# Linear attention with a highway feed-forward: the key turns moved a whole iteration ahead of their scores, to the head of the TensorE sequence

## The chip, the cores and the metric

The kernel runs on one core of a Trainium2 chip. The time is that of the device in microseconds (us), from runs of the whole program; the profile comes from one further execution. TensorE (PE) multiplies matrices into PSUM, VectorE (DVE) and ScalarE (ACT) read PSUM and write SBUF, GpSimd (POOL) works in SBUF alone, and SyncE (SP) issues the DMAs. Each engine takes its instructions in the sequence in which the program wrote them, and waits for the others on semaphores.

## The reference

Attention with a decay per head, in blocks, and behind it a highway layer. Cut to what matters (q, k, v are 4 x 8 x 768 x 64, 3072 tokens of width 512):

```python
for b in range(nb):
    intra = einsum(qb, kb) * Dmask          # lam ** (i - j) where i >= j
    intra = einsum(intra, vb)
    inter = einsum(qb * lam_pow, kv_state)
    out[b] = intra + inter
    kv_state = lam_block * kv_state + einsum(kb * rev_pow, vb)
x = out.transpose(0, 2, 1, 3).reshape(B * S, H * D)
H = maximum(x @ w_h, 0)
T = 1 / (1 + exp(-(x @ w_t + b_t)))
return T * H + (1 - T) * x
```

Inputs and output are float32; the kernel multiplies in bf16.

## The kernel before, in words

**Tiling.** The kernel takes chunks of 128 tokens with all eight heads: 24 chunks (N), six for each of the four batch entries (NCH). The powers of the decay are not in the masks: V is scaled by a power for its position (`scale_v`, L143), the result by one for the query's position (`intra`, L202), so the mask is a plain triangle. Two chunks form a group of 256 tokens for the feed-forward; the last two chunks are groups of their own.

**Steps of a chunk n.** POOL casts the keys to bf16 (`cast_k`, L138) and scales V (L145); queries are cast for two chunks at a time (`cast_q`, L153). PE turns the keys, four 128x128 transposes into the PSUM tile "tr" (`trans_k`, L166), and ACT copies them to `kT` (L168). Queries go the same way for two chunks at a time, eight transposes into a tile of the same name and one ACT copy (`trans_q`, L159 and L161). Both share the one PSUM buffer of "tr". `scores` (L179) multiplies turned queries and keys, eight matmuls, and DVE masks the result (L182). `inter` (L189) is the product with the state so far, four matmuls, left out for the first chunk of a batch entry; `intra` (L196) adds the masked scores times V, eight matmuls, and DVE writes the result as xT (L202). `state` (L211) updates the state with four matmuls, and ACT copies it in two halves to `s_bd` (L215); it is left out for the last chunk of a batch entry.

**Feed-forward.** A group is worked off in two units of half the output columns. `ffn_step` takes one unit: eight matmuls for H (`h_ps`, L223; DVE makes hmx from it, L226), then, if a finished chunk waits, its output (`ffn_out`: eight matmuls into `x_ps`, L250, an ACT copy to `o_sb`, L254, and a DMA, L257), then eight matmuls for T (`t_ps`, L235), two sigmoids on ACT (L239) and a DVE product (`thmx`, L242). PSUM has one buffer for each of these tiles.

**Sequence.** The sequence is the one in which the code is written; there is no scheduler. The first two chunks are worked off ahead of the loop, with the two units of the first group. Iteration i of the loop holds: POOL's casts for chunk i + 3; inter(i); scores(i + 1); intra(i) and state(i); in even iterations the query turns for chunks i + 2 and i + 3; one `ffn_step`; the key turns for chunk i + 2; the loads for chunk i + 10. The scores of chunk i + 2 stand in iteration i + 1, with inter(i + 1) alone between the turns and them on PE. From iteration 24 on there are only feed-forward units and outputs left.

**Buffers.** Loads have ten buffers for each of k and v and five for the query pairs; `kb` and `vs` four, `kT` three, `qT` and `qb` two, `o_sb` six.

Of the kernel before, what the change touches and what calls it, by code (L numbers as in the profile page):

```python
# [16 lines left out]
def kernel(  # L17
# [19 lines left out]
    N = B * NCH  # L37
# [100 lines left out]
    def cast_k(n, eng=None):  # L138
        kb[n] = work.tile([C, H, D], BF16, tag="kb", name="kb", bufs=4)
        (eng or nc.gpsimd).tensor_copy(kb[n], kf[n])  # L140

    def scale_v(n):
        c = n % NCH  # L143
        vs[n] = work.tile([C, H, D], BF16, tag="vs", name="vs", bufs=4)
        nc.gpsimd.tensor_tensor(vs[n], in0=vf[n], in1=pow_k[:, :, c, :].to_broadcast([C, H, D]), op=ALU.mult)  # L145

    def cast_q(s, engs=None):
        qb[s] = work.tile([128, J, H, D], BF16, tag="qb", name="qb")
        engs = engs or [nc.gpsimd]
        w = H // len(engs)  # L150
        for i, eng in enumerate(engs):
            h = slice(i * w, i * w + w)
            eng.tensor_copy(qb[s].rearrange("p j h d -> p h j d")[:, h], qf[s].rearrange("p h (j d) -> p h j d", j=J)[:, h])  # L153

    def trans_q(s):
        tr = ps.tile([128, NP, J, 128], BF16, tag="tr", name="tr")
        for hp in range(NP):
            for j in range(J):
                nc.tensor.transpose(tr[:, hp, j, :], qb[s][:, j, 2 * hp:2 * hp + 2, :], id128)  # L159
        qT[s] = work.tile([128, NP, J * C], BF16, tag="qT", name="qT")  # L160
        nc.scalar.activation(qT[s].rearrange("p n (q j) -> p n q j", j=J), tr.rearrange("p n j q -> p n q j"), AF.Copy)  # L161

    def trans_k(n):
        tr = ps.tile([128, NP, C], BF16, tag="tr", name="tr")
        for hp in range(NP):
            nc.tensor.transpose(tr[:, hp, :], kb[n][:, 2 * hp:2 * hp + 2, :], id128)  # L166
        kT[n] = work.tile([128, NP, C], BF16, tag="kT", name="kT", bufs=3)
        nc.scalar.activation(kT[n], tr, AF.Copy)  # L168

    def q_of(n, r, hp):  # L170
        o = n % J * C
        return qT[n // J][r, hp, o:o + C]

    def scores(n):
        s_ps = ps.tile([C, 2, NP, C], F32, tag="s", name="s_ps")
        for hp in range(NP):
            for e in range(2):
                r = slice(64 * e, 64 * e + 64)
                nc.tensor.matmul(s_ps[:, e, hp, :], lhsT=kT[n][r, hp, :], rhs=q_of(n, r, hp), start=True, stop=True)  # L179
        masked[n] = work.tile([C, 2, NP, C], BF16, tag="masked", name="masked")  # L180
        for e in range(2):
            nc.vector.tensor_tensor(masked[n][:, e], in0=s_ps[:, e],  # L182
                                    in1=tri.to_broadcast([C, NP, C]), op=ALU.mult)

    def inter(n):
        o_ps[n] = ps.tile([128, NP, C], F32, tag="o", name="o_ps")
        if n % NCH:
            for hp in range(NP):
                nc.tensor.matmul(o_ps[n][:, hp, :], lhsT=s_bd[n % 2][:, hp, :], rhs=q_of(n, slice(0, 128), hp),  # L189
                                 start=(hp == 0), stop=False, skip_group_check=True)  # L190

    def intra(n):
        c = n % NCH
        for hp in range(NP):
            for e in range(2):
                nc.tensor.matmul(o_ps[n][64 * e:64 * e + 64, hp, :], lhsT=vs[n][:, 2 * hp + e, :], rhs=masked[n][:, e, hp, :],  # L196
                                 start=(hp == 0 and c == 0), stop=True, skip_group_check=True)
        g = group[n]
        r = n - first[g]
        if r == 0:  # L200
            xT[g] = work.tile([128, NP, sizes[g] * C], BF16, tag=f"xT{sizes[g]}", name="xT", bufs=3)
        nc.vector.tensor_tensor(xT[g][:, :, r * C:(r + 1) * C], in0=o_ps[n], in1=pow_q[:, :, c * C:(c + 1) * C], op=ALU.mult)  # L202

    def state(n):
        b, c = divmod(n, NCH)
        if c == NCH - 1:
            return
        if c == 0:
            kv_ps[b] = ps.tile([128, NP, 128], F32, tag="kv", name="kv_ps")
        for hp in range(NP):  # L210
            nc.tensor.matmul(kv_ps[b][:, hp, :], lhsT=kb[n][:, 2 * hp:2 * hp + 2, :], rhs=vs[n][:, 2 * hp:2 * hp + 2, :],  # L211
                             start=(c == 0 and hp == 0), stop=True, skip_group_check=True)
        for e in range(2):
            r = slice(64 * e, 64 * e + 64)
            nc.scalar.activation(s_bd[(n + 1) % 2][r, :, r], kv_ps[b][r, :, r], AF.Copy)  # L215


    def ffn_h(g, js):
        T = sizes[g] * C
        h_ps = ps.tile([128, len(js), T], F32, tag="h", name="h_ps")  # L220
        for i, j in enumerate(js):
            for kc in range(KC):
                nc.tensor.matmul(h_ps[:, i, :], lhsT=wh[:, kc, j * 128:(j + 1) * 128], rhs=xT[g][:, kc, :],  # L223
                                 start=(kc == 0), stop=(kc == KC - 1))
        hmx = work.tile([128, len(js), T], BF16, tag=f"hmx{len(js)}", name="hmx")
        nc.vector.scalar_tensor_tensor(hmx, in0=h_ps, scalar=0.0, in1=xT[g][:, js[0]:js[-1] + 1, :],  # L226
                                       op0=ALU.max, op1=ALU.subtract)
        return hmx

    def ffn_t(g, js, hmx):  # L230
        T = sizes[g] * C
        t_ps = ps.tile([128, len(js), T], F32, tag="t", name="t_ps")
        for i, j in enumerate(js):
            for kc in range(KC):
                nc.tensor.matmul(t_ps[:, i, :], lhsT=wt[:, kc, j * 128:(j + 1) * 128], rhs=xT[g][:, kc, :],  # L235
                                 start=(kc == 0), stop=(kc == KC - 1))
        t_sb = work.tile([128, len(js), T], BF16, tag=f"t_sb{len(js)}", name="t_sb")
        for i, j in enumerate(js):
            nc.scalar.activation(t_sb[:, i, :], t_ps[:, i, :], AF.Sigmoid, bias=bt_col[:, j:j + 1])  # L239
        if js[0] == 0:  # L240
            thmx[g] = work.tile([128, NP, T], BF16, tag=f"thmx{sizes[g]}", name="thmx")
        nc.vector.tensor_tensor(thmx[g][:, js[0]:js[-1] + 1, :], in0=t_sb, in1=hmx, op=ALU.mult)  # L242

    def ffn_out(n, eng="act"):
        g = group[n]
        r = n - first[g]
        x_ps = ps.tile([C, DM], F32, tag="x", name="x_ps")
        for j in range(NP):
            for i, t in enumerate((xT[g], thmx[g])):
                nc.tensor.matmul(x_ps[:, j * 128:(j + 1) * 128], lhsT=t[:, j, r * C:(r + 1) * C], rhs=id128,  # L250
                                 start=(j == 0 and i == 0), stop=(i == 1), skip_group_check=True)
        o_sb = work.tile([C, DM], F32, tag="o_sb", name="o_sb", bufs=6)
        if eng == "act":
            nc.scalar.activation(o_sb, x_ps, AF.Copy)  # L254
        else:
            nc.vector.tensor_copy(o_sb, x_ps)  # L256
        nc.sync.dma_start(out=out[n * C:(n + 1) * C, :], in_=o_sb)  # L257
# [3 lines left out]
    def ffn_step(eng="act"):  # L261
        unit = units.pop(0) if units else None
        if unit:
            hmx = ffn_h(*unit)
        if outs:
            ffn_out(outs.pop(0), eng)
        if unit:
            ffn_t(*unit, hmx)
            g, js = unit
            if js[-1] == NP - 1:  # L270
                outs.extend(range(first[g], first[g] + sizes[g]))
# [31 lines left out]
    cast_q(1)  # L303
    scale_v(2)
    ffn_step()
    ffn_step()
    trans_k(2)
    trans_q(1)
    scores(2)
    cast_k(3)  # L310
    scale_v(3)
# [8 lines left out]
    i = 2  # L320
    while i < N or units or outs:
        if i + 3 < N:
            cast_k(i + 3)
            scale_v(i + 3)
            if i % J and (i + 3) % J == 0:
                cast_q((i + 3) // J)
        if i < N:
            inter(i)
        if i + 1 < N:
            scores(i + 1)  # L330
        if i < N:
            intra(i)
            state(i)
        if i % J == 0 and i + 2 < N:
            trans_q(i // J + 1)
        ffn_step("dve" if i >= N and i % 2 else "act")
        if i < N:
            close(i)
        if i + 2 < N:
            trans_k(i + 2)  # L340
        loads(i + LA)
        i += 1

# [29 lines left out]
```

## Time and profile before

| | us |
|---|---|
| median of 3 runs (lowest to highest) | 141.66 (141.54 to 141.77) |
| the profiled execution | 141.39 |
| its span, from the first to the last instruction | 139.6 |
| PE busy | 102.9 |
| ACT busy | 81.2 |
| DVE busy | 77.8 |
| POOL busy | 55.3 |

The mean granted TensorE clock was 0.959 of full speed. The kernel moved 27.48 MB. The span is shorter than the profiled execution's time by 1.8 us, which lie around the first and the last instruction. A row of the timeline gives start, duration, engine, line and operation, what it writes and reads, how many such instructions are merged in the row, and in brackets the engine's idle time ahead of it with what ended it. Matmul durations include the pipeline's depth, so that the pitch of a series is read from start to start.

### The profile page before, as it was taken

What the parts mean: (1) busy time and instruction counts of PE and PEld (TensorE: products, weight loads), DVE (VectorE), ACT (ScalarE), POOL (GpSimd) and SP (SyncE); (2) the same over time, 40 slices, a digit from 0 to 9 for tenths busy, and PEclk for the clock granted to TensorE, in tenths of its full rate; (3) what the DMA queues carried; (4) which work ended last, traced back from release to release, by engine and by line L of the source; (5) the groups of instructions that cost most, each with busy time, mean ns of one, the idle gap of its engine ahead of it and who ended that gap; (6) DMA issues with size and microseconds to landing.
All of it is one profiled execution on the core that took longest, in us unless ns stands there. A gap on an engine that the chain in (4) does not pass through costs nothing.

```text
span 139.6 us, 3394 instructions
## 1 busy us (share of the span) xinstructions
PE 102.9 (74%) x1345; PEld 85.8 (61%) x1345; DVE 77.8 (56%) x135; ACT 81.2 (58%) x165; POOL 55.3 (40%) x73
## 2 busy tenths in 40 slices
PE   0257893789976887797779779778867977799950
PEld 0144572577755775686568569557756865688840
DVE  4316832625657595476477447645854774674351
ACT  3756946184543855846656567559368566745540
POOL 5076357382919391545336237337325400000000
PEclk9999999655899999999999999999999999999998
DMA  1999999999998999999999999998122022102323
GB/s 41 275 257 368 303 233 236 217 217 243 246 219 210 247 275 260 225 258 258 288 267 262 254 267 261 270 284 241 50 80 75 0 75 80 71 6 86 144 79 146
DMA packets 67175, 27.48 MB, mean 197 GB/s; under 512 B 50772, under 2 KB 63064, under 8 KB 67160
## 3 DMA queue, kind: packets, MB, share of 16 engines
q1 hardware_dynamic: 67008, 27.27, 81.4%
q8 instruction: 10, 0.16, 0.5%
q14 instruction: 5, 0.04, 0.1%
q10 hardware_dynamic: 152, 0.01, 0.1%
HBM read 20.98 MB, written 6.29 MB: 195 GB/s over the span
## 4 chain that ended last, share of the span: by engine, by line
PE 60%; ACT 24%; DVE 6%; DMA 4%; issue 3%; SPq 0%; ACTq 0%
PE t_ps L235 15%; PE h_ps L223 14%; ACT t_sb L239 13%; ACT kT L168 8%; PE s_ps L179 8%; PE x_ps L250 7%; PE o_ps L196 6%; PE kv_ps L211 5%; PE tr L159 5%; DMA qf<-in_q_dram 4%; DVE masked L182 3%; ACT qT L161 2%; DVE o_sb L256 1%; ACT o_sb L254 1%; DVE w_b L294 1%
## 5 line engine op out<-in xcount | busy, mean ns | idle before, releaser
L182 DVE TENSOR_TENSOR masked<-s_ps,tri 128x512 bf16<-128x512 f32 x48 | 30.9, 686 | 19.9 <-PE s_ps L179 19.6
L145 POOL TENSOR_TENSOR vs<-vf,pow_k 128x512 bf16<-128x512 f32 x24 | 25.6, 1067 | 18.0 <-DMA vf<-in_v_dram 10.2
L215 ACT ACTIVATE s_bd<-kv_ps 64x256 bf16<-64x256 f32 x40 | 15.1, 378 | 25.8 <-PE kv_ps L211 25.3
L242 DVE TENSOR_TENSOR thmx<-t_sb,hmx 128x512 bf16<-128x512 bf16 x24 | 11.0, 459 | 30.7 <-ACT t_sb L239 30.7
L239 ACT ACTIVATE t_sb<-t_ps,bt_col 128x256 bf16<-128x256 f32 (+1 forms) x52 | 20.8, 455 | 11.7 <-PE t_ps L235 11.7
L179 PE MATMUL s_ps<-qT,kT 64*128 64x128 bf16 x192 | 10.6, 236 | 21.9 <-ACT kT L168 18.8
L223 PE MATMUL h_ps<-xT,w_b 128*128 128x256 bf16 (+1 forms) x208 | 25.8, 270 | 0.4 <-DVE xT L202 0.4
L235 PE MATMUL t_ps<-xT,w_b 128*128 128x256 bf16 (+1 forms) x208 | 25.5, 268 | 0.1
L140 POOL CAST kb<-kf 128x512 bf16<-128x512 f32 x23 | 14.1, 614 | 26.7 <-issue 18.0
L179 PEld LDWEIGHTS <-kT 64*128 64x128 bf16 x192 | 6.2, 101 | 26.1 <-ACT kT L168 23.5
L223 PEld LDWEIGHTS <-w_b 128*128 128x128 bf16 x208 | 18.5, 100 | 2.8 <-issue 0.6
L235 PEld LDWEIGHTS <-w_b 128*128 128x128 bf16 x208 | 18.7, 100 | 2.2 <-issue 0.2
L254 ACT ACTIVATE o_sb<-x_ps 128x512 f32<-128x512 f32 x22 | 13.1, 595 | 9.9 <-PE x_ps L250 9.8
L226 DVE SCALAR_TENSOR_TENSOR hmx<-h_ps,xT 128x512 bf16<-128x512 f32 x24 | 16.4, 684 | 2.3 <-PE h_ps L223 1.5
L202 DVE TENSOR_TENSOR xT<-o_ps,pow_q 128x512 bf16<-128x512 f32 x24 | 16.3, 680 | 0.7 <-PE o_ps L196 0.7
L153 POOL CAST qb<-qf 128x1024 bf16<-128x1024 f32 (+1 forms) x12 | 12.5, 1040 | 7.7 <-DMA qf<-in_q_dram 7.7
L250 PE MATMUL x_ps<-id,xT 128*128 128x128 bf16 x96 | 14.2, 227 | 1.3 <-ACT o_sb L254 0.7
L168 ACT ACTIVATE kT<-tr 128x512 bf16<-128x512 bf16 x24 | 14.3, 596 | 1.2 <-PE tr L166 1.1
L250 PE MATMUL x_ps<-id,thmx 128*128 128x128 bf16 x96 | 14.2, 227 | 0.2 <-DVE thmx L242 0.2
L161 ACT ACTIVATE qT<-tr 128x1024 bf16<-128x1024 bf16 x12 | 12.3, 1024 | 2.7 <-PE tr L159 2.4
L196 PE MATMUL o_ps<-masked,vs 128*64 128x128 bf16 x192 | 11.4, 241 | 0.8 <-DVE masked L182 0.8
L250 PEld LDWEIGHTS <-thmx 128*128 128x128 bf16 x96 | 9.8, 102 | 2.1 <-DVE thmx L242 1.2
(42 smaller groups left out, 97.9 us busy)
## 6 DMA issues: line engine op xcount, KB each, us to landing
kf<-in_k_dram SPq DMA_DIRECT2D x24, 256.0 KB, 4.9
qf<-in_q_dram SPq DMA_DIRECT2D x12, 512.0 KB, 5.7
vf<-in_v_dram SPq DMA_DIRECT2D x24, 256.0 KB, 5.7
out_dram<-o_sb SPq DMA_DIRECT2D x24, 256.0 KB, 4.5
w_f<-in_moe_w_h_dram SPq DMA_DIRECT2D x4, 256.0 KB, 4.5
w_f<-in_moe_w_t_dram SPq DMA_DIRECT2D x4, 256.0 KB, 5.3
lam_bc<-in_lam_dram ACTq DMA_DIRECT2D x1, 4.0 KB, 3.1
bt_r<-in_moe_b_t_dram ACTq DMA_DIRECT2D x1, 2.0 KB
```

What stands on the lines that cost most here:

```text
L145: nc.gpsimd.tensor_tensor(vs[n], in0=vf[n], in1=pow_k[:, :, c, :].to_broadcast([C, H, D]), op=ALU.mult)
L168: nc.scalar.activation(kT[n], tr, AF.Copy)
L179: nc.tensor.matmul(s_ps[:, e, hp, :], lhsT=kT[n][r, hp, :], rhs=q_of(n, r, hp), start=True, stop=True)
L182: nc.vector.tensor_tensor(masked[n][:, e], in0=s_ps[:, e], in1=tri.to_broadcast([C, NP, C]), op=ALU.mult)
L196: nc.tensor.matmul(o_ps[n][64 * e:64 * e + 64, hp, :], lhsT=vs[n][:, 2 * hp + e, :], rhs=masked[n][:, e, hp, :], start=(hp == 0 and c == 0 ...
L202: nc.vector.tensor_tensor(xT[g][:, :, r * C:(r + 1) * C], in0=o_ps[n], in1=pow_q[:, :, c * C:(c + 1) * C], op=ALU.mult)
L215: nc.scalar.activation(s_bd[(n + 1) % 2][r, :, r], kv_ps[b][r, :, r], AF.Copy)
L223: nc.tensor.matmul(h_ps[:, i, :], lhsT=wh[:, kc, j * 128:(j + 1) * 128], rhs=xT[g][:, kc, :], start=(kc == 0), stop=(kc == KC - 1))
L226: nc.vector.scalar_tensor_tensor(hmx, in0=h_ps, scalar=0.0, in1=xT[g][:, js[0]:js[-1] + 1, :], op0=ALU.max, op1=ALU.subtract)
L235: nc.tensor.matmul(t_ps[:, i, :], lhsT=wt[:, kc, j * 128:(j + 1) * 128], rhs=xT[g][:, kc, :], start=(kc == 0), stop=(kc == KC - 1))
L239: nc.scalar.activation(t_sb[:, i, :], t_ps[:, i, :], AF.Sigmoid, bias=bt_col[:, j:j + 1])
L250: nc.tensor.matmul(x_ps[:, j * 128:(j + 1) * 128], lhsT=t[:, j, r * C:(r + 1) * C], rhs=id128, start=(j == 0 and i == 0), stop=(i == 1), s ...
```

## The change

Two calls move. In the loop, the key turns of chunk i + 2 (`trans_k(i + 2)`) stood behind the feed-forward unit of iteration i, and now stand at its head, ahead of inter(i). The scores of chunk i + 2 stay in iteration i + 1. Ahead of the loop, the turns of keys 2 and of the second query pair stood behind the two feed-forward units of the first group, and now stand between them.

```diff
     scale_v(2)
     ffn_step()
-    ffn_step()
     trans_k(2)
     trans_q(1)
+    ffn_step()
     scores(2)
...
                 cast_q((i + 3) // J)
+        if i + 2 < N:
+            trans_k(i + 2)
         if i < N:
             inter(i)
         if i + 1 < N:
...
         if i < N:
             close(i)
-        if i + 2 < N:
-            trans_k(i + 2)
         loads(i + LA)
```

PE in the steady loop, before: the end of iteration 7 and iteration 8 up to its query turns. One row stands for each series of four or eight matmuls. Numbers tell the buffers apart: kb_686 holds the keys of chunk 9, kT_860 their turned copy, made from tr_855.

```order
L235 MATMUL t_ps_842<-xT_562,w_b1_90 128x256
L166 MATMUL tr_855<-id128_135,kb_686 128x128
L189 MATMUL o_ps_870<-qT_729,s_bd0_158 128x128
L179 MATMUL s_ps_875<-qT_729,kT_860 128x128
L196 MATMUL o_ps_870<-masked_801,vs_621 64x128
L211 MATMUL kv_ps_713<-vs_621,kb_619 128x128
L159 MATMUL tr_903<-id128_135,qb_785 128x128
```

The same place after the change; the keys of chunk 9 (kb_686) were turned at the head of iteration 7, which is the row at the top, and kb_781 holds those of chunk 10.

```order
L166 MATMUL tr_787<-id128_135,kb_686 128x128
L235 MATMUL t_ps_849<-xT_569,w_b1_90 128x256
L166 MATMUL tr_870<-id128_135,kb_781 128x128
L189 MATMUL o_ps_877<-qT_736,s_bd0_158 128x128
L179 MATMUL s_ps_882<-qT_736,kT_792 128x128
L196 MATMUL o_ps_877<-masked_808,vs_621 64x128
L211 MATMUL kv_ps_720<-vs_621,kb_619 128x128
L159 MATMUL tr_910<-id128_135,qb_785 128x128
```

The series have the same sequence of kinds here; what moved is the chunk that is turned. Iteration 8's scores read kT_792, turned in iteration 7's head, and the turns that stand in front of them are for the scores of iteration 9.

ACT at the same place, before and then after:

```order
L239 ACTIVATE t_sb_851<-t_ps_842,bt_col_171 128x256 x2
L168 ACTIVATE kT_860<-tr_855 128x512
L215 ACTIVATE s_bd1_160<-kv_ps_713 64x4x64 x2
L161 ACTIVATE qT_912<-tr_903 128x1024
L254 ACTIVATE o_sb_934<-x_ps_925 128x512
```

```order
L239 ACTIVATE t_sb_858<-t_ps_849,bt_col_171 128x256 x2
L168 ACTIVATE kT_875<-tr_870 128x512
L215 ACTIVATE s_bd1_160<-kv_ps_720 64x4x64 x2
L161 ACTIVATE qT_919<-tr_910 128x1024
L254 ACTIVATE o_sb_941<-x_ps_932 128x512
```

ACT's sequence of kinds is the same in the loop; the key copy behind the sigmoids is that of chunk 10 and no longer that of chunk 9. DVE, POOL and SP have the same sequences before and after.

## Prediction

> **What bounds the kernel now.** I read the page first, for what is busy and what the chain that ended last is made of. Rows of section 2 (40 slices of 3.5 us: TensorE busy, granted TensorE clock, DMA) and of section 4:
>
> ```profile
> PE   0257893789976887797779779778867977799950
> PEclk9999999655899999999999999999999999999998
> DMA  1999999999998999999999999998122022102323
> PE 60%; ACT 24%; DVE 6%; DMA 4%; issue 3%; SPq 0%; ACTq 0%
> ```
>
> No engine is full. The DMA engines are loaded until slice 27 (about 97 us) and nearly idle afterwards, yet PE shows the same 7 to 8 tenths before and after that point: in the second half it isn't the loads that hold PE. ACT carries 24% of the chain. The view of waits says where PE stops for ACT:
>
> ```profile
> PE s_ps L179 <- ACT kT L168: 18.8, 20, 1.2
> ```
>
> The scores wait 20 times for the copy of the turned keys. One iteration of the loop shows how. PE from the timeline (start, duration, engine, line; matmuls are pipelined, so I count from start to start), then ACT in the same stretch:
>
> ```profile
> 54.97 0.61 PE L159 MATMUL tr<-id,qb 128*128 128x128 bf16 x8
> 55.41 1.04 PE L223 MATMUL h_ps<-xT,w_b 128*128 128x256 bf16 x8
> 56.29 0.22 PE L250 MATMUL x_ps<-id,xT 128*128 128x128 bf16 x1
> ...
> 56.73 1.04 PE L235 MATMUL t_ps<-xT,w_b 128*128 128x256 bf16 x8
> 57.61 0.39 PE L166 MATMUL tr<-id,kb 128*128 128x128 bf16 x4
> 57.83 0.39 PE L189 MATMUL o_ps<-qT,s_bd 128*128 128x128 bf16 x4
> 59.19 0.40 PE L179 MATMUL s_ps<-qT,kT 64*128 64x128 bf16 x8 [0.97 <-ACT kT L168]
> 59.52 0.41 PE L196 MATMUL o_ps<-masked,vs 128*64 128x128 bf16 x8
> 59.86 0.40 PE L211 MATMUL kv_ps<-vs,kb 128*128 128x128 bf16 x4
> 60.10 1.04 PE L223 MATMUL h_ps<-xT,w_b 128*128 128x256 bf16 x8
> ```
>
> ```profile
> 57.81 0.84 ACT L239 ACTIVATE t_sb<-t_ps,bt_col 128x256 bf16<-128x256 f32 x2 [0.26 <-PE t_ps L235]
> 58.54 0.60 ACT L168 ACTIVATE kT<-tr 128x512 bf16<-128x512 bf16 x1
> ```
>
> PE turns the keys at 57.61 and runs the state product at 57.83; those four matmuls end their issue at about 58.05 (four of them took 0.22 at 57.61). ACT is busy with two sigmoids until 58.65, then copies kT until 59.14, and the scores start at 59.19. So PE issues nothing for 59.19 - 58.05 = 1.14 us in each iteration. The path is PE's FFN, ACT's sigmoids, ACT's kT, PE's scores, and round again.
>
> Up to about 50 us something else holds too. POOL's casts of the queries (start, duration; the first row is the scaling of V ahead of one):
>
> ```profile
> 34.35 1.06 POOL L145 TENSOR_TENSOR vs<-vf,pow_k 128x512 bf16<-128x512 f32 x1 [2.55 <-DMA vf<-in_v_dram]
> 35.35 1.04 POOL L153 CAST qb<-qf 128x1024 bf16<-128x1024 f32 x1
> 42.67 1.04 POOL L153 CAST qb<-qf 128x1024 bf16<-128x1024 f32 x1
> 49.34 1.23 POOL L153 CAST qb<-qf 128x1024 bf16<-128x1024 f32 x1
> ```
>
> POOL waits for V there, and the pairs of queries are ready at 36.39, 43.71 and 50.57, 7.3 and 6.9 us apart. No order on PE brings these forward.
>
> **The pre-loop edit** puts the second pair's turns between the two FFN units. PE's waits there now, and the cast that iteration 2 needs:
>
> ```profile
> 22.78 0.61 PE L159 MATMUL tr<-id,qb 128*128 128x128 bf16 x8 [1.19 <-ACT kT L168]
> 24.50 0.40 PE L179 MATMUL s_ps<-qT,kT 64*128 64x128 bf16 x8 [1.11 <-ACT qT L161]
> ```
>
> ```profile
> 26.88 1.04 POOL L153 CAST qb<-qf 128x1024 bf16<-128x1024 f32 x1 [2.14 <-DMA qf<-in_q_dram]
> ```
>
> The second unit's matmuls would lie beside these copies, so up to 2.3 us of waits can go. I cost it at nothing, because the query turns of iteration 2 need the cast that ends at 27.92, and those of iteration 4 the one that ends at 36.39: what is gained ahead is waited away there.
>
> **The loop edit** moves four turns per iteration and one ACT copy; it adds and removes no instruction, and neither SP's, POOL's nor DVE's sequence changes. The scores of iteration i now read a kT copied a whole iteration earlier, so the 1.14 us goes. What is late next, in the order of the iteration, counted from the turns at its head:
>
> PE's own pitch, from the rows above: turns 0.22, state product 0.22, scores 0.33, intra 0.34, state update 0.24, h 0.88, x 0.44, t 0.88, together 3.55 us; the query turns of even iterations 0.44.
>
> The turned tiles share one PSUM buffer ("tr", one buffer). The query turns now come 1.35 us after the key turns (0.22 + 0.22 + 0.33 + 0.34 + 0.24), and the kT copy ends 59.14 - 57.61 = 1.53 after them, since ACT still does the sigmoids first; with 0.05 to pass the signal (59.14 to 59.19) the query turns can start at 1.58. So 0.23 of the wait comes back in each even iteration. This is a new wait, and h, x and t stand behind it. An even iteration is then 1.58 + 0.44 + 0.88 + 0.44 + 0.88 = 4.22, a pair 7.77. Where a chunk is the last of its batch the state update (0.24) is left out, in odd iterations only; where it is the first, the state product is left out, which the new wait swallows.
>
> VectorE, from the same stretch:
>
> ```profile
> 59.63 1.29 DVE L182 TENSOR_TENSOR masked<-s_ps,tri 128x512 bf16<-128x512 f32 x2 [0.52 <-PE s_ps L179]
> 60.84 0.68 DVE L202 TENSOR_TENSOR xT<-o_ps,pow_q 128x512 bf16<-128x512 f32 x1
> 61.43 0.68 DVE L226 SCALAR_TENSOR_TENSOR hmx<-h_ps,xT 128x512 bf16<-128x512 f32 x1
> 63.36 0.42 DVE L242 TENSOR_TENSOR thmx<-t_sb,hmx 128x512 bf16<-128x512 bf16 x1 [1.25 <-ACT t_sb L239]
> ```
>
> After the change the sigmoids end 1.04 after the head (57.81 + 0.84 - 57.61); thmx then ends at 1.46, masked at 2.75, xT at about 3.4, hmx at about 4.0. The next state product needs xT's PSUM tile at 3.55 + 0.22 = 3.77: 0.4 us of slack. The next h, at 3.55 + 1.35 = 4.9, needs hmx: 0.9. So DVE does not bind, but the first margin is small. ACT: the kT copy is done by 1.53, before the state update's result can arrive; its longest sequence in an even iteration ends before the next sigmoids.
>
> **The sum.** Iteration 4's query turns start when their cast is done, 36.39 and 0.05 for the signal, say 36.45. From there to those of iteration 6 PE has 0.44 + 0.88 + 0.88 (no x yet), an iteration without state update and x, 2.87, and 1.58: 43.10, and it waits for the cast until 43.76. To iteration 8: 2.64 + 3.55 + 1.58, so 51.53, now behind PE and not behind the cast (50.57). Before, this point was 54.97: 3.44 gained. From there to the start of h in iteration 22, the last with scores: six pairs less two state updates, 6 x 7.77 - 0.48 = 46.14, then 2.64 + 3.55 and 1.13 (no turns in iteration 22), 53.46 together. It starts at 104.99. Before:
>
> ```profile
> 123.21 1.04 PE L223 MATMUL h_ps<-xT,w_b 128*128 128x256 bf16 x8
> ```
>
> That is 18.2 us earlier, and behind it the same work follows as before (16.4 us to the end of the span, 139.6). The profiled execution took 141.39, so 123.2; the median of the runs is 141.66, 0.27 above it: 123.4.
>
> Does the DMA allow it? SP's issues in sequence, and the time to landing:
>
> ```profile
> 62.41 0.59 SPq L55 DMA_DIRECT2D kf<-in_k_dram  x1
> 88.14 1.52 SPq L60 DMA_DIRECT2D vf<-in_v_dram  x1
> 89.75 1.05 SPq L257 DMA_DIRECT2D out_dram<-o_sb  x1
> 90.89 0.39 SPq L55 DMA_DIRECT2D kf<-in_k_dram  x1
> ```
>
> ```profile
> vf<-in_v_dram SPq DMA_DIRECT2D x24, 256.0 KB, 5.7
> out_dram<-o_sb SPq DMA_DIRECT2D x24, 256.0 KB, 4.5
> ```
>
> SP issues without a pause here: seven chunks with their outputs in 90.89 - 62.41 = 28.48 us, 4.07 each, slower than the 3.85 that PE would now take. PE starts with a lead to spend. The queries for iteration 20 come after the V issued at 88.14: 93.8 landed, 1.06 and 1.04 on POOL, 95.9; PE wants them at 51.53 + 46.14 = 97.7. The output buffers (six) tell the same: the o_sb of iteration 19 needs the output issued at 89.75 gone, 94.3, and ACT wants it at about 95.4. Margins of 1 to 2 us: the loads nearly bind, and a floor follows. At 95.9 instead of 97.7 the whole would be 121.6.
>
> **The clock.** The granted clock in stretches (fields: window, length, busy of PE, PEld, DVE, ACT, POOL, clock, DMA share, GB/s):
>
> ```profile
> 24.00:26.00 2.00, 0.95 (x16) 0.67 (x15) 1.06 (x2) 1.05 (x2) 0.73 (x2) 0.94 1.17 256
> 34.00:36.00 2.00, 1.66 (x22) 1.20 (x22) 0.19 (x1) 1.08 (x2) 1.65 (x2) 0.50 1.33 217
> 36.00:38.00 2.00, 2.00 (x31) 1.74 (x26) 1.72 (x4) 1.29 (x3) 2.00 (x4) 1.00 1.12 254
> ```
>
> PE ran at half clock from about 26 to 36 us, and came back as FFN matmuls began. After the change PE waits for the cast of 36.39. If the half clock of some 9.5 us fell behind that wait, it would cost 4.7 us of work, less the 0.66 in hand before 43.76: about 4.1. If it stays ahead of it, nothing. I take 0.9, nearer to nothing, because in the trace the clock is back at once with the FFN. Sum: 124.3.
>
> The Trainium skill (TensorE: Matmul & The Clock Gate, "HAM oscillation — how this bites in real kernels") says that an idle gap of PE of over about 3.4 us drops the clock to half; this speaks against the change, which makes PE reach its wait sooner. By that page, as an estimate, one window of 3.4 us at half clock behind the wait would lose 1.7 us of work, and the sum would be 124.4 rather than the 123.4 without any loss. The 0.50 at 34 to 36 us agrees with a halved clock; that the waits quoted ahead of it are 1.19 us at most doesn't.
>
> **Rivals.**
> *The DMA becomes the bound* (15 in 100). For it: 4.07 against 3.85, margins under 2 us. Against: what is issued, and in which sequence, stays. If the loads from 51 us on came a tenth slower, the last queries would be 4.4 us later, 100.3 instead of 97.7 wanted; with the 0.9 about 127, and with outputs delayed likewise up to 130.
> *Half of the wait returns elsewhere* (12 in 100): in-line waits on ACT or DVE, such as xT's with its 0.4 us of slack. 14 iterations x 0.57 = 8 us: 132.
> *The wait isn't worth its time* (2 in 100): another round (sigmoid, thmx, masked, xT) has the same length and takes its place. Then about 141.6. The DVE's 0.52 and 1.25 us of idle time in that round speak against it.
> *Slower* (3 in 100): PE reaches waits for loads so often that the clock stays at half. An iteration then takes about 3.85 longer. The gain of 18.2 is lost when 18.2 / 3.85, some five iterations, run so, that is 37 us at half clock beyond those of now. From 36 to 85 us it would cost 24: about 148. The clock of 1.00 with waits of 1.14 us per iteration now speaks against it.
>
> **How the numbers follow.** The forecast has 68 in 100, 124.3, and by itself spans 122 to 126.5 (no clock term and loads at their floor, to most of the 4.1). With the DMA rival the range is 122 to 130 for 83 in 100. Faster by over 0.2% (what a measurement here can tell): 68 + 15 + 12 = 95; within it 2; slower 3.
>
> **What would show it.** The next query turns of before, for the pitch:
>
> ```profile
> 64.78 0.61 PE L159 MATMUL tr<-id,qb 128*128 128x128 bf16 x8
> ```
>
> Right: the wait of the scores for kT is gone (18.8 us to under 3); a new one of the query turns for kT of about 0.2 in each even iteration; pairs of iterations of about 7.7 us where 9.8 stood (54.97 above to the row below); h of iteration 22 near 105; the last key load issued at about 91 as now. Wrong: waits of PE for POOL's kb or qb behind 51 us (the DMA rival), waits for xT (the second), or 0.50 in the clock row behind 40 us (the last).

## The result and the profile after

The changed kernel took 125.66 us in the median of 4 runs (124.51 to 126.75), beside 141.6 for the kernel before; the ratio is 0.885, with a 95% interval of 0.877 to 0.893. The profiled execution took 125.1 us with a span of 123.3. A second series gave 126.03 in the median of 6 (ratio 0.887, 0.882 to 0.891). The prediction said 124.3, with a range of 122 to 130. Ratios and their intervals leave out runs over 1.5% slower than the fastest of the same kernel; the medians count every run.

The same rows of the page as shown of before (TensorE busy, granted clock, DMA, by engine on the chain that ended last):

```profile
PE   0236896756819999999999999999999999999930
PEclk9999999999985999999999999999999999999996
DMA  1999999998999999899999999999999972222233
PE 57%; SPq 18%; DMA 8%; ACT 6%; DVE 4%; issue 2%; POOL 2%; POOLq 0%
```

PE is now at 9 tenths from slice 13 (from about 37 us) to slice 38 (about 117 us), where it stood at 7 to 8. ACT has gone from 24% of the chain to 6%. What holds the end now is PE's own sequence behind about 37 us, and ahead of it the loads, which stand as SPq and DMA. In the view of waits, over the whole span, those of PE for casts and for turned copies:

```profile
PE tr L159 <- POOL qb L153: 3.4, 2, 2.5
PE tr L159 <- ACT kT L168: 1.7, 4, 1.2
PE s_ps L179 <- ACT qT L161: 1.1, 1, 1.1
```

The 18.8 us of the scores waiting for kT are gone altogether. The 1.1 us of the last row and 1.2 of the 1.7 us for kT stand ahead of the loop. Inside it, query turns wait for the cast (0.85 and 2.51 us), and three times, up to 0.19 us, for the kT copy to leave the shared PSUM buffer. One pair of iterations on PE, from the timeline:

```profile
52.59 0.61 PE L159 MATMUL tr<-id,qb 128*128 128x128 bf16 x8
...
55.22 0.39 PE L166 MATMUL tr<-id,kb 128*128 128x128 bf16 x4
55.45 0.39 PE L189 MATMUL o_ps<-qT,s_bd 128*128 128x128 bf16 x4
55.77 0.40 PE L179 MATMUL s_ps<-qT,kT 64*128 64x128 bf16 x8
56.09 0.41 PE L196 MATMUL o_ps<-masked,vs 128*64 128x128 bf16 x8
...
58.87 0.39 PE L166 MATMUL tr<-id,kb 128*128 128x128 bf16 x4
...
60.45 0.61 PE L159 MATMUL tr<-id,qb 128*128 128x128 bf16 x8
...
63.08 0.39 PE L166 MATMUL tr<-id,kb 128*128 128x128 bf16 x4
```

The scores start 0.32 us behind the state product, without a wait. The odd iteration takes 58.87 - 55.22 = 3.65, the even one 63.08 - 58.87 = 4.21, the pair 7.86, where it was 9.8. The query turns come 60.45 - 58.87 = 1.58 behind the key turns, as forecast for the shared buffer.

The steps of the sum against two profiles of the changed kernel (in brackets with the clock term of 0.9):

| start, us | forecast | first profile | second profile |
|---|---|---|---|
| query turns, iteration 4 | 36.45 | 36.58 | 36.65 |
| query turns, iteration 6 | 43.76 (44.66) | 44.73 | 44.31 |
| query turns, iteration 8 | 51.53 (52.43) | 52.59 | 52.19 |
| query turns, iteration 20 | 97.67 (98.57) | 99.46 | 99.77 |
| h, iteration 22 | 104.99 (105.89) | 106.97 | 107.28 |
| end of the span | 121.4 (122.3) | 123.3 | 123.6 |

At iteration 8 the sum with the clock term holds to 0.25 us; at iteration 6 it is 0.07 short in the first profile and 0.35 long in the second, where the clock did not fall. From iteration 8 to iteration 22 it is short by 0.9 in the first profile and 1.6 in the second.

### The profile page after: what moved, and what is told of

The parts are those of the page before. It is cut to its first block, busy times and chain, and to the rows that moved or that the text cites. A ratio compares the mean times of both kernels' runs of the same rounds, so it can differ in the third digit from the quotient of the medians.

```text
span 123.3 us, 3388 instructions
## 1 busy us (share of the span) xinstructions
PE 101.0 (82%) x1345; PEld 84.1 (68%) x1345; DVE 79.5 (64%) x135; ACT 81.9 (66%) x165; POOL 56.4 (46%) x73
## 4 chain that ended last, share of the span: by engine, by line
PE 57%; SPq 18%; DMA 8%; ACT 6%; DVE 4%; issue 2%; POOL 2%; POOLq 0%
PE h_ps L223 14%; PE t_ps L235 14%; SPq L60 9%; PE x_ps L250 7%; SPq L55 6%; DMA vf<-in_v_dram 5%; PE tr L159 5%; PE o_ps L196 4%; ACT t_sb L239 4%; PE s_ps L179 4%; DMA w_f<-in_moe_w_h_dram 4%; PE kv_ps L211 3%; PE o_ps L189 3%; SPq L65 2%; PE tr L166 2%
## 5 line engine op out<-in xcount | busy, mean ns | idle before, releaser
L242 DVE TENSOR_TENSOR thmx<-t_sb,hmx 128x512 bf16<-128x512 bf16 x24 | 15.4, 643 | 21.1 <-ACT t_sb L239 20.9
L223 PE MATMUL h_ps<-xT,w_b 128*128 128x256 bf16 (+1 forms) x208 | 26.7, 276 | 0.2 <-POOL w_b L300 0.2
L223 PEld LDWEIGHTS <-w_b 128*128 128x128 bf16 x208 | 18.8, 101 | 2.9 <-issue 0.4
L235 PEld LDWEIGHTS <-w_b 128*128 128x128 bf16 x208 | 18.9, 100 | 2.2
L153 POOL CAST qb<-qf 128x1024 bf16<-128x1024 f32 (+1 forms) x12 | 13.1, 1088 | 8.0 <-DMA qf<-in_q_dram 8.0
L250 PE MATMUL x_ps<-id,xT 128*128 128x128 bf16 x96 | 13.4, 219 | 1.3 <-ACT o_sb L254 0.7
L250 PE MATMUL x_ps<-id,thmx 128*128 128x128 bf16 x96 | 13.4, 219 | 0.2 <-DVE thmx L242 0.2
L159 PE MATMUL tr<-id,qb 128*128 128x128 bf16 x96 | 8.2, 233 | 6.3 <-POOL qb L153 3.4
L159 PEld LDWEIGHTS <-qb 128*128 128x128 bf16 x96 | 6.6, 103 | 7.9 <-POOL qb L153 4.5
L166 PE MATMUL tr<-id,kb 128*128 128x128 bf16 x96 | 9.8, 227 | 2.3 <-DVE kb L140 0.8
L179 PE MATMUL s_ps<-qT,kT 64*128 64x128 bf16 x192 | 10.0, 226 | 2.0 <-ACT qT L161 1.1
```

## The experiments

Medians are of 6 runs (12 of the pre-loop edit alone), ratios are to the kernel before on the same chip, with 95% intervals. The second series of the changed kernel ran on one chip with three of the others: queries cast ahead, query turns behind h, first outputs left out. Kernels from different chips are compared by their ratios.

| kernel | us | ratio |
|---|---|---|
| the changed kernel, second series | 126.03 | 0.887 (0.882 to 0.891) |
| loop edit alone | 125.63 | 0.884 (0.880 to 0.889) |
| pre-loop edit alone | 142.41 | 0.999 (0.995 to 1.003) |
| turns half an iteration ahead | 127.81 | 0.897 (0.892 to 0.903) |
| PE's wait filled | 125.35 | 0.882 (0.876 to 0.888) |
| queries cast ahead of V's scaling | 124.91 | 0.877 (0.872 to 0.882) |
| query turns behind h | 123.26 | 0.866 (0.862 to 0.871) |
| first outputs left out | 125.15 | 0.881 (0.877 to 0.884) |
| twelve output buffers | 125.25 | 0.879 (0.874 to 0.885) |
| query turns behind h, twelve output buffers | 122.91 | 0.864 (0.859 to 0.868) |
| the three together | 121.49 | 0.853 (0.848 to 0.859) |
| V not scaled from chunk 12 on | 126.01 | 0.883 (0.877 to 0.889) |

**The changed kernel again.** No edit.

> The changed kernel itself once more, as the measure for the runs beside it: 125.7 within 0.8.

126.03. In this profile the clock stayed at full rate throughout, and yet the end is no earlier. The view of waits, then the place in ACT's timeline and the query turns of iteration 20 on PE:

```profile
ACT o_sb L254 <- DMA out_dram<-o_sb: 3.2, 2, 1.8
```

```profile
97.90 0.60 ACT L254 ACTIVATE o_sb<-x_ps 128x512 f32<-128x512 f32 x1 [1.80 <-DMA out_dram<-o_sb]
```

```profile
99.77 0.61 PE L159 MATMUL tr<-id,qb 128*128 128x128 bf16 x8 [0.85 <-ACT kT L168]
```

ACT waits 1.8 us for an output DMA to leave its buffer; the sigmoids and the kT copy stand behind that on ACT, and the query turns behind the kT copy. The output buffers, for which the forecast had 1 to 2 us in hand, do bind here. In the first profile, where the clock cost some time earlier, no such wait stands. Of these two executions, one lost time to the clock and the other to the outputs.

**The loop edit alone.** The pre-loop sequence is that of before:

```diff
     ffn_step()
+    ffn_step()
     trans_k(2)
     trans_q(1)
-    ffn_step()
```

> The loop edit alone; ahead of the loop the sequence of before. My theory: what the pre-loop edit gains is waited away at the query cast that ends at 36.4, so the time is that of the changed kernel, 125.7 within 0.8, and iteration 4's query turns start at about 36.6 as in it. Rival: the pre-loop edit carries some of the gain (its two waits are 2.3 us): then 127 to 128. A second rival: without the second unit's matmuls between the turns the clock falls earlier, as in the kernel before (half from 26 us), and the half-clock stretch no longer lies behind 36.6: then up to 1 us faster.

125.63: the same time. Iteration 4's query turns start at 36.78, in the changed kernel at 36.58.

**The pre-loop edit alone.** The kernel before, with the opposite edit.

> The pre-loop edit alone; in the loop the sequence of before. My theory: no difference that can be measured against the kernel before (141.6 within 0.4), since iteration 4's query turns still wait for the same cast. Rival: it is worth up to 2.3 us, 139.3.

The ratio is 0.999 (0.995 to 1.003): no difference. The two runs together agree with the step "what is gained ahead is waited away there". The second rival of the first run isn't borne out either: its clock did fall earlier, to 0.50 at 28 to 30 us, and it was no faster.

**Turns half an iteration ahead.** The kernel before, with one move:

```diff
         if outs:
             ffn_out(outs.pop(0), eng)
+        if between:
+            between()
         if unit:
...
-        ffn_step("dve" if i >= N and i % 2 else "act")
+        ffn_step("dve" if i >= N and i % 2 else "act",
+                 (lambda: trans_k(i + 2)) if i + 2 < N else None)
         if i < N:
             close(i)
-        if i + 2 < N:
-            trans_k(i + 2)
```

> The kernel before, with the key turns half an iteration ahead: between the output's matmuls and the t product of the same feed-forward step, so that ACT copies kT ahead of the two sigmoids and not behind them; the scores still read it in the next iteration. My theory: the wait of 1.14 us per iteration is the two sigmoids (0.84) ahead of the copy on ACT, so that a place ahead of the sigmoids is enough: the scores' wait falls from 18.8 us to under 4, and the time is 125 to 129 (in even iterations the key turns wait up to 0.4 for the query copy in the shared PSUM buffer). Rival: it takes the whole iteration's distance: then the wait stays at over 10 us, and the time is over 134.

127.81, so 14 of the 16 us come with this alone. The waits of the scores and of the key turns in its profile:

```profile
PE s_ps L179 <- ACT kT L168: 0.8, 2, 0.5
PE tr L166 <- ACT qT L161: 2.0, 9, 0.3
```

The scores' wait has gone from 18.8 to 0.8 us with the scores in the same iteration behind the turns as in the kernel before; the whole iteration of distance isn't needed. But the edit does two things at once: the copy comes ahead of the two sigmoids on ACT, and the t product, 0.88 us, comes between the turns and the scores. The two were not tried apart. How long a copy takes that nothing on ACT delays can be read in the changed kernel, ahead of its loop (PE, then ACT):

```profile
24.57 0.40 PE L166 MATMUL tr<-id,kb 128*128 128x128 bf16 x4 [0.76 <-ACT kT L168]
25.07 0.60 ACT L168 ACTIVATE kT<-tr 128x512 bf16<-128x512 bf16 x1 [0.55 <-PE tr L166]
```

It ends 1.10 us behind the start of the turns. In the kernel before, with turns at 57.61 and 0.05 us for the signal, the scores could then have started at 58.76 in place of 59.19. By this estimate the sigmoids make 0.43 of the 1.14 us, and the other 0.71 is the copy's own way, which only distance takes off. The key turns wait for the query copy in the shared buffer, nine times up to 0.3, about as expected.

**PE's wait filled.** Ten matmuls more in iteration 4:

```diff
+        if i == 4:
+            fill = ps.tile([C, DM], F32, tag="x", name="fill")
+            for _ in range(10):
+                nc.tensor.matmul(fill, lhsT=id128, rhs=wh[:, 0, :], start=True, stop=True)
         if i % J == 0 and i + 2 < N:
             trans_q(i // J + 1)
```

> The changed kernel, with ten 128x512 matmuls on data that lie in SBUF, into a PSUM tile that nobody reads, in iteration 4 ahead of the query turns, where PE waits 2.5 us for the cast. It adds work and takes none away. My theory: PE's clock falls to half from 36 to 39.4 us because PE idles there, and this costs about 1 us: with the fill the clock is at 1.00 from 36 to 40, iteration 6's query turns come near 43.8 and no longer at 44.7, and the time is 0.7 to 1 us less than that of the changed kernel, about 124.8. Rival: the clock falls for another reason, or the loss is regained at the next wait for a cast: the same time or up to 0.5 more.

The stretch of 34 to 40 us, first the changed kernel in its first profile, then in its second, then with the fill (the field behind POOL's is the clock):

```profile
34.00:36.00 2.00, 0.07 (x2) 0.00 (x0) 1.33 (x3) 0.76 (x2) 1.52 (x2) 1.00 1.28 228
36.00:38.00 2.00, 1.42 (x11) 1.28 (x12) 0.00 (x0) 0.35 (x1) 1.69 (x3) 0.52 0.84 190
38.00:40.00 2.00, 2.00 (x14) 1.46 (x12) 0.65 (x1) 0.67 (x1) 0.99 (x2) 0.63 1.25 281
```

```profile
34.00:36.00 2.00, 1.07 (x22) 0.70 (x20) 1.56 (x3) 1.05 (x3) 1.44 (x2) 1.00 1.37 225
36.00:38.00 2.00, 1.35 (x17) 1.26 (x18) 0.33 (x1) 0.69 (x1) 2.00 (x3) 1.00 1.10 220
```

```profile
34.00:36.00 2.00, 1.95 (x19) 1.03 (x15) 1.76 (x3) 0.76 (x2) 1.11 (x2) 1.00 1.15 204
36.00:38.00 2.00, 1.67 (x18) 1.05 (x16) 0.00 (x0) 0.35 (x1) 1.58 (x3) 1.00 0.98 205
```

With the fill the clock holds and iteration 6's query turns start at 44.12 and iteration 8's at 51.99, 0.6 earlier than in the first profile. But the clock also holds in the second profile, without any fill: there PE reaches this place later and waits 1.58 us in place of 2.51. Two other runs are much the same up to this place and wait as long, first outputs left out (2.64 us) and V not scaled (2.66). Their clock falls to half here as well, and their query turns of iteration 6 come at 44.98 and 46.14. Where the wait is 1.39 and 1.46 us, with the loop edit alone and with twelve output buffers, the clock holds at this place. So in these profiles the half clock goes with the long wait at this place, as the theory had it, and iteration 6 is then 0.4 to 1.8 us behind the second profile's 44.31. The time, 125.35, can't be told from 126.03 or 125.66: the expected 0.7 to 1 us of the median is not shown.

**Queries cast ahead of V's scaling.**

```diff
             cast_k(i + 3)
-            scale_v(i + 3)
             if i % J and (i + 3) % J == 0:
                 cast_q((i + 3) // J)
+            scale_v(i + 3)
```

> The changed kernel, with POOL casting the queries of a pair ahead of scaling the V that is loaded behind them (two steps of POOL swapped in odd iterations). My theory: up to iteration 6 PE is held by the query cast, and that by the V ahead of it on POOL: the cast of iteration 4's queries ends near 34.4 and no longer at 36.5, PE's long wait there is gone and with it some of the half clock, and the time is 1.5 to 3 us less, 122.7 to 124.2. Rival: the loads bind right behind (the output buffers or the queries of iteration 20): the gain is given back later and the time is within 0.5 of the changed kernel's.

124.91, 1.1 below the changed kernel beside it; the intervals just touch. The query turns of iteration 4 come at 34.83 in place of 36.65, those of iteration 8 at 50.84 in place of 52.19. In the kept profile it is then given back; in the view of waits

```profile
ACT o_sb L254 <- DMA out_dram<-o_sb: 8.6, 6, 2.2
```

This profiled execution was 1.2 us above its median, so the 8.6 shows the kind of the wait and not its usual size. By the medians 1.1 us of the gain stays. The theory's start came true, and the time lies between the theory's (122.7 to 124.2) and the rival's (within 0.5 of the changed kernel).

**Query turns behind h.** In `ffn_step` the turns stand between h and the output's matmuls:

```diff
         if unit:
             hmx = ffn_h(*unit)
+        if between:
+            between()
         if outs:
...
-        if i % J == 0 and i + 2 < N:
-            trans_q(i // J + 1)
-        ffn_step("dve" if i >= N and i % 2 else "act")
+        ffn_step("dve" if i >= N and i % 2 else "act",
+                 (lambda: trans_q(i // J + 1)) if i % J == 0 and i + 2 < N else None)
```

> The changed kernel, with the query turns of even iterations behind the h product and no longer ahead of it, so that the kT copy has long left the PSUM buffer which both turns share. My theory: the changed kernel's even iterations wait 0.13 for that buffer (4.21 measured against 4.09 for the matmuls alone), seven of them, and some 0.3 where the state product is left out: 0.8 to 1.2 us less, about 124.7. Rival: the query copy then pushes the output copy and the sigmoids on ACT, 0.3 later per even iteration, thmx and xT follow on VectorE and the next state product waits for xT: the same time or up to 1 us more.

123.26: 2.8 less than the changed kernel, more than double what was expected. PE's timeline in the front part:

```profile
34.64 1.04 PE L223 MATMUL h_ps<-xT,w_b 128*128 128x256 bf16 x8
36.81 0.62 PE L159 MATMUL tr<-id,qb 128*128 128x128 bf16 x8 [1.14 <-POOL qb L153]
...
42.74 1.04 PE L223 MATMUL h_ps<-xT,w_b 128*128 128x256 bf16 x8
44.22 0.62 PE L159 MATMUL tr<-id,qb 128*128 128x128 bf16 x8 [0.44 <-POOL qb L153]
```

The h product, 0.88 us, now runs while PE would have waited for the cast. That is the part I had not counted: the key turns of iteration 9, which have the same work ahead of them in both kernels, start at 53.73, against 54.82 in the second profile of the changed kernel, 1.1 earlier (54.24 and 0.6 in the profile with twelve buffers, below). From there to h of iteration 22 (104.91 against 107.28) it gains 1.3 more. 0.4 of that is a shorter wait behind the outputs at iteration 20 (0.47 in place of 0.85 us); the rest, 0.9, is the part that was expected. The rival's loss on ACT didn't show.

**First outputs left out.** The output DMAs of chunks 0 to 11 are not issued:

```diff
-        nc.sync.dma_start(out=out[n * C:(n + 1) * C, :], in_=o_sb)
+        if n >= 12:
+            nc.sync.dma_start(out=out[n * C:(n + 1) * C, :], in_=o_sb)
```

> The changed kernel without the output DMAs of the first 12 chunks (those 12 chunks of the output are left out), so that the DMA carries 3.1 MB less while loads are still under way. My theory: behind 52 us PE's own sequence is the bound, the loads have 1 to 2 us in hand: the loads end several us earlier, and the time moves by less than 0.5. Rival: the loads and output buffers bind from 60 us on: the time falls by 1.5 us or more.

125.15. The last key load is issued at 87.25 us, in the changed kernel beside it at 92.57, and no output buffer is waited for. With over 5 us of relief for the loads the time falls by 0.9 with overlapping intervals. The loads and outputs together are a bound at the edge, worth about 1 us at most in the changed kernel.

**Twelve output buffers.**

```diff
-        o_sb = work.tile([C, DM], F32, tag="o_sb", name="o_sb", bufs=6)
+        o_sb = work.tile([C, DM], F32, tag="o_sb", name="o_sb", bufs=12)
```

> The changed kernel with twelve output buffers in place of six. My theory, after the runs before: where the clock stays at full rate, PE comes early enough that ACT waits for an output DMA to leave its buffer (3.2 us in two waits in the second profile of the changed kernel), and this takes back 0.85 us at iteration 20; with twelve buffers these waits are gone, and the time is 0.3 to 1 us less than the changed kernel's 126.0. Rival: the end is bound by the outputs' DMAs themselves, which are then late all the same: no difference.

125.25; the waits for output buffers are gone, but the interval overlaps that of six buffers. In its profile iteration 20's query turns come at 98.91 and wait 0.2 for the cast, ahead of which POOL waited 4.05 us for its V: the loads are next at once.

> Query turns behind h as in the earlier run of that edit, and twelve output buffers. My theory: ACT's waits for output buffers (4.9 us in three waits there) are gone, iteration 20's query turns wait 0.47 less, and the time is 0.5 to 1.5 us less than with six buffers (123.3): about 122.3. Rival: no difference, as above.

122.91 beside 123.26: no difference that can be told. With query turns behind h the buffers matter little.

**The three together.** Queries cast ahead, query turns behind h, twelve buffers.

> Queries cast ahead of V's scaling on POOL, query turns behind h, and twelve output buffers. My theory: swapping the casts gained 1.7 us at iteration 8 and lost it to the output buffers (8.6 us of ACT waits); with the buffers there it is kept, and the time is 120 to 122, the fastest of all. Rival: the loads then bind (queries of iteration 20): no faster than query turns behind h with twelve buffers.

121.49, ratio 0.853 (0.848 to 0.859): 14.7% below the kernel before and about 4.5 us below the changed one, the fastest here. Its query turns of iterations 4, 8 and 20 start at 35.57, 50.29 and 95.96, and no wait for output buffers is listed. Beside query turns behind h with twelve buffers the intervals touch, the medians differ by 1.4.

**V not scaled from chunk 12 on.**

```diff
     def scale_v(n):
         c = n % NCH
+        if n >= 12:
+            vs[n] = vs[n - 4]
+            return
```

> The changed kernel without scaling V for chunks 12 to 23 on POOL (they read the scaled V of chunks 8 to 11 instead; that part of the computation is left out). It is to show why VectorE's thmx takes 0.42 us at times and up to 1.24 at others in the changed kernel. My theory: it is held up while POOL works on SBUF beside it: in the second half, where POOL has only casts left, its mean falls from 0.74 to under 0.55, and the time moves by under 0.5. Rival: the length comes from something else (PE's or the DMA's traffic): thmx stays as long as it was.

126.01. The groups of thmx between 70 and 100 us, the changed kernel in its first profile, in its second, and then this one:

```profile
L242 DVE TENSOR_TENSOR thmx<-t_sb,hmx 128x512 bf16<-128x512 bf16 x8 | 5.7, 714 | 6.8 <-ACT t_sb L239 6.7
L242 DVE TENSOR_TENSOR thmx<-t_sb,hmx 128x512 bf16<-128x512 bf16 x8 | 4.6, 571 | 8.3 <-ACT t_sb L239 8.3
```

```profile
L245 DVE TENSOR_TENSOR thmx<-t_sb,hmx 128x512 bf16<-128x512 bf16 x7 | 3.6, 520 | 7.5 <-ACT t_sb L242 7.5
```

The mean is under 0.55, as expected, and the time doesn't move. But the changed kernel itself has 0.71 in one execution and 0.57 in another, so that the mean alone shows little. What settles it is which operations meet, and that follows in the last section.

## Why the prediction was right, point by point

**The wait that goes.** "So the 1.14 us goes": shown. The scores wait for kT nowhere in the profile after, and the run with turns half an iteration ahead shows that half the distance does it too. In the changed kernel ACT still copies behind the sigmoids, so there it is the distance alone that took the wait away.

**The pre-loop edit at nothing.** Shown by the two halves run alone.

**The loads hold the front.** Shown: the query turns of iteration 4 start 0.13 later than forecast, and they move by 1.1 to 1.8 us when POOL casts the queries ahead of V's scaling.

**The new wait in the shared buffer.** Right in size: the query turns stand 1.58 behind the key turns in forecast and trace, even iterations 4.22 forecast and 4.21 measured. The wait in it is 0.13 and not 0.23 us, since PE's own work up to it takes 1.45 (55.22 to 56.67) and not 1.35.

**PE's own pitch.** Here the sum was short. "State product 0.22" was taken from the four key turns, and the scores were put right behind it. In the steady loop of the kernel before, the wait for kT lay over this place. Its last iteration has no scores, and there two rows show 0.31 from the state product to the next series, intra:

```profile
125.41 0.39 PE L189 MATMUL o_ps<-qT,s_bd 128*128 128x128 bf16 x4
125.72 0.41 PE L196 MATMUL o_ps<-masked,vs 128*64 128x128 bf16 x8
```

So a sign of it could be read beforehand. After the change the scores start 0.32 behind the state product (55.45 to 55.77 above). That makes an odd iteration 3.65 and not 3.55; in even ones the wait in the shared buffer takes it up. With seven odd iterations behind iteration 8 and iteration 22 itself, 8 x 0.10 = 0.8 us: most of the 0.9 by which the first profile is late there.

**VectorE's small margin.** Forecast at 0.4 us, "so DVE does not bind". It did once behind 36 us in the first profile; the chain that ended last, at iteration 20:

```profile
95.15 1.24 DVE thmx L242
96.39 1.20 DVE masked L182 x2
97.58 0.61 DVE xT L202
98.23 0.38 PE o_ps L189 x4
```

thmx takes 1.24 in place of 0.42, and the state product waits for xT until 98.23, about 0.3 us. The wait in the shared buffer would have taken part of that up: this pair is 0.17 longer than the others (99.46 - 91.43 = 8.03, not 7.86). The step failed in taking thmx's length as fixed.

**The DMA.** "The loads nearly bind": shown. The last key load is issued at 92.09 and 92.57, against about 91 forecast; the output buffers bind in the second profile (0.85 us at iteration 20), and take back part of what casting the queries earlier gains. The DMA rival was priced at about 127 and more; what the runs show is its beginning, up to 1 us.

**The clock.** Taken at 0.9 in a range of 0 to 4.1. The first profile has half clock from 36 to about 39.5 us and iteration 6 is late by 0.97; the second has none. Its iteration 6 is late by 0.55 for another reason: POOL's cast ends at 44.25 there, not at 43.71. That the sum with the clock term holds at iteration 8 in both is in part luck. As a term of the median it isn't settled. The rule of the Trainium skill (TensorE: Matmul & The Clock Gate, "HAM oscillation — how this bites in real kernels") is to leave no gap of PE of over about 3.4 us; here the clock fell behind a wait of 2.5 us (34 to 36 us: PE busy for 0.07 of 2), and in the run with the loop edit alone at 28 us, with PE busy for 1.25 of the 2 us ahead of it. The measurements decide: a shorter wait among light work is enough.

Together: pitch 0.8, and 0.17 from VectorE in the first profile or 0.85 from the outputs in the second, account for the 0.9 and 1.6 us behind iteration 8, and by their size for the 1.4 us between 124.3 and 125.66. That the median of runs moved by exactly these terms can't be shown from two profiles; the runs spread over 2.2 us.

## What to carry to other kernels

Where PE waits for a copy by an engine that also does other work, look at what stands ahead of that copy in its in-order sequence: here two sigmoids (0.84 us) and the copy itself (0.60) left PE waiting for 1.14 us per iteration, and moving the producer ahead, by half an iteration or a whole one, was worth 10 to 12%. A row measured next to a wait hides the pitch at the place of the wait, so allow for it in the sum. When a wait goes, work that needs no load belongs in front of the next one: the query turns behind h were worth 2.8 us more, and in the profiles 0.6 to 1.1 us of that came because h ran ahead of that wait.

## What the runs showed of the hardware

**VectorE held up by POOL.** thmx reads two operands in SBUF. Of the changed kernel, thmx on VectorE, then POOL at the same places:

```profile
64.16 1.17 DVE L242 TENSOR_TENSOR thmx<-t_sb,hmx 128x512 bf16<-128x512 bf16 x1 [1.09 <-ACT t_sb L239]
87.51 0.42 DVE L242 TENSOR_TENSOR thmx<-t_sb,hmx 128x512 bf16<-128x512 bf16 x1 [1.26 <-ACT t_sb L239]
90.93 1.02 DVE L242 TENSOR_TENSOR thmx<-t_sb,hmx 128x512 bf16<-128x512 bf16 x1 [0.60 <-ACT t_sb L239]
```

```profile
64.01 1.04 POOL L153 CAST qb<-qf 128x1024 bf16<-128x1024 f32 x1
...
87.83 1.06 POOL L145 TENSOR_TENSOR vs<-vf,pow_k 128x512 bf16<-128x512 f32 x1 [3.03 <-PE o_ps L196]
...
90.61 1.06 POOL L145 TENSOR_TENSOR vs<-vf,pow_k 128x512 bf16<-128x512 f32 x1 [0.18 <-PE s_ps L179]
```

Where POOL began first, thmx ends 0.28 us behind POOL's end: 65.33 and 65.05, 91.95 and 91.67, and likewise 96.39 and 96.11 at iteration 20. Where thmx began first (87.51) it takes 0.42. VectorE's other operations in the loop have one operand in PSUM and keep their length (xT 678 ns in the mean, 680 before). With V's scaling left out, the long ones that remain stand behind casts: 81.06 to 81.87 behind a cast of queries that ends at 81.59, again 0.28. This agrees with the Trainium skill (SBUF — State Buffer, "Who interferes with whom"): a VectorE instruction with two SBUF inputs takes its second through a read interface that it shares with GpSimd; the shared ports are an exclusive lock, and the order of issue decides who waits.

**A longer hand-over between series of matmuls.** Four matmuls of 128 columns take 0.22 us up to the next series whose stationary tiles are 128 x 128 too. Up to the scores, whose stationary tiles have 64 rows, they take 0.32, and 0.31 to 0.32 up to intra, whose stationary tiles have 64 columns (125.41 to 125.72 before, 109.16 to 109.48 after). What makes the 0.10 wasn't tried.
